# A fused attention and two-layer MLP kernel: the first block's work in another written order

## The chip, the core and the metric

The kernel runs on one core of one Trainium2 chip. The metric is the device time of one execution in microseconds (us), a median over runs. The profiles shown here are each of one execution, and times in them count from the start of its span.

## The reference

```python
def _attn_ref(q, k, v, alpha):                 # q, k, v, alpha: [4, 8, 768, 48]
    for t in range(S):
        state = alpha[:, :, t, :, None] * state + np.einsum('bhd,bhe->bhde', k[:, :, t], v[:, :, t])
        y[:, :, t] = np.einsum('bhd,bhde->bhe', q[:, :, t], state)

def reference(**kwargs):
    x = attention output as [3072 tokens, 384]
    h = x @ w_in                               # [384, 2048]
    x = (h * sigmoid(1.702 * h)) @ w_out       # layer 1
    h = x @ w_in2
    return (h - np.tanh(h)) @ w_out2           # layer 2
```

A linear attention with a decay per channel feeds two MLP layers. The inputs are drawn as float64, and the MLP weights reach the device as 64-bit numbers.

## The kernel before

**Tiles.** Tokens go through each layer in six blocks of 512. The hidden width 2048 is sixteen tiles of 128, numbered m. In one step of a block, `gemm1` (g) makes a hidden tile from the block's tokens, ScalarE applies the gate (`sig_1`, s), and `gemm2` (u) adds the gated tile's share to three accumulating banks of PSUM. Every factor is kept as a high part that TensorE multiplies in one pass and a low remainder, so that each product is three matmuls: a `gemm1` and a `gemm2` are nine matmuls of 128x512 each.

**Gate.** `g_hi` (i) copies the gated tile to its high part on ScalarE, and the low part is the gated tile less the high part: `g_lo` (f) on VectorE. For tiles 6 to 15 of the first block the kernel before uses `g_add` instead: ScalarE writes the negated high part, and an accumulating DMA issued by GpSimd adds the gated tile to it. There are three buffers each for the gated tile, its high and its low part, and two banks of PSUM for `gemm1`.

**Weights.** The weights of hidden tile m (input and output columns together, 768 KB) come by `w_given(m)` (w) on SyncE's DMA queue. They are converted on the device: `w_bits` (b, two VectorE instructions, L172 and L173) and `w_join` (j, L185) build a float32 number, `w_hi` (H, ScalarE, L204) writes the high part and `w_lo` (L, VectorE, L208) the low part. Five buffers (`cf` and two in `xs`) hold the float32 numbers. Layer 1's weights are converted once, all during the first block.

**Attention.** It works in chunks of 128 tokens, 24 in all. Chunks 0 to 3 make the first block's tokens and run ahead of it. Chunks 4 to 7 make the second block's tokens and are worked off between the steps of the first block; for each of them VectorE runs two scans (`a_scan`, p and q), two products (`a_scale`, k) and the state's update (`a_state`, t), TensorE the scores (`s_mm`, S, two halves), the outputs and the state's step (`a_out`, O), ScalarE copies (`s_copy`, `a_guard` d), and GpSimd a masking select for each half of the scores (L310). `a_done` (E) copies the outputs out of PSUM, sends them to memory and reads them back turned (`a_evac`, `a_back`), and then issues the loads of the chunk three further on. `x_hi` and `x_lo` (X, x) split what was read back into the factors of `gemm1`. The later chunks run inside the general loop, whose step s does `gemm1(s)` and `gemm2(s - 3)`.

**Order.** Each engine works off its instructions in the order in which the program is written, up to the last block of layer 1 (`in_order`). A DMA queue's instructions stand in the order of the engine that issues them. In the first block a list of words sets the order: each word is a letter of the table `part` and a number, `g7` being `gemm1` of tile 7. In the list before, the conversion of tile m + 2 or so stands in a row, b, j, H and L one behind the other, next to the step of tile m.

Of the kernel before, what the change touches and what calls it, by code (L numbers as in the profile page):

```python
# [7 lines left out]
F32 = mybir.dt.float32  # L8
# [4 lines left out]
AF = mybir.ActivationFunctionType  # L13
ALU = mybir.AluOpType
# [3 lines left out]
C = 128  # L18
# [50 lines left out]
def linear_attention_mlps(ctx, tc, xq, xv, fa, fv, cst, w1, w2, out):  # L69
    nc = tc.nc  # L70
    V, A, G, P, SP = nc.vector, nc.scalar, nc.gpsimd, nc.tensor, nc.sync
# [22 lines left out]
    glo = [T(f"glo{i}", (128, NB), F32R) for i in range(3)]  # L94
# [28 lines left out]
    for _ in range(2):  # L123
        t = carve(QW)
# [21 lines left out]
    bank = [ps.tile([128, 512], F32, name=f"bank{i}") for i in range(8)]  # L146
# [14 lines left out]
    def w_given(m):  # L161
        SP.dma_start(out=given[m], in_=w1[m].bitcast(I32).rearrange("p (n t) -> p n t", t=2))
# [105 lines left out]
    def a_guard(g):  # L268
        t = (gt if g == 2 else rawf if place_of(g) is spare else arena[:, (QW + VW) * late.index(place_of(g)) :])[:DP, : 2 * AW]
        A.activation(out=t, in_=t, func=AF.Square, accum_out=guard[:, g : g + 1])  # L270
# [157 lines left out]
    def a_back(g):  # L428
        _, xl, o = a_at(g)
        tk = slice(g * C, g * C + C)  # L430
        SP.dma_start(out=xl[:, :, o].bitcast(F32), in_=xt.rearrange("h d t -> (h d) t")[:, tk].rearrange("(k p) t -> p k t", p=128))
# [4 lines left out]
    def x_hi(g, t=None):  # L436
        xh, xl, o = a_at(g)
        A.copy(xh[:, :, o], xl[:, :, o].bitcast(F32) if t is None else x_of(g, t))  # L438

    def x_lo(g, t=None):  # L440
        xh, xl, o = a_at(g)
        V.tensor_tensor(out=xl[:, :, o], in0=xl[:, :, o].bitcast(F32) if t is None else x_of(g, t), in1=xh[:, :, o].bitcast(F32), op=ALU.subtract)  # L442
# [21 lines left out]
    HB = [bank[3], bank[4]]  # L464
# [3 lines left out]
    def gb(s):  # L468
        return gf[s % turn[0]]

    def sig_1(s, h, n):
        A.activation(out=gb(s)[:, :n], in_=h, func=AF.Silu, scale=1.702)  # L472

    def g_hi(s, n):
        A.copy(ghi[s % 3][:, :n], gb(s)[:, :n])  # L475

    def g_lo(s, n):
        V.tensor_tensor(out=glo[s % 3][:, :n], in0=gb(s)[:, :n], in1=ghi[s % 3][:, :n].bitcast(F32), op=ALU.subtract)  # L478

    def g_add(s, n):  # L480
        A.activation(out=glo[s % 3][:, :n], in_=gb(s)[:, :n], func=AF.Copy, scale=-1.0)  # L481
        G.dma_start(out=glo[s % 3][:, :n].bitcast(F32), in_=gb(s)[:, :n], accum_op=ALU.add)

    def g_split(s, n):
        g_hi(s, n)
        g_lo(s, n)
# [49 lines left out]
    LAG = 3  # L536
# [115 lines left out]
    for g in range(3):  # L652
        for r in range(3):
            prep(g + 1, r)
        if g < 2:
            for r in range(2):
                s_mm(g + 1, r, (5, 3)[r])
        if g:
            a_state(g - 1)
        if g < 2:  # L660
            a_out(g, 0)
            idle((4, 3)[g])
        else:
            a_out(2, 0, part=0)
            for r in range(2):
                s_mm(3, r, (5, 3)[r])
            a_out(2, 0, part=1)
        for x in range(2):
            s_copy(g + 1, x, (5, 3)[x], False)
        if g == 2:  # L670
            a_take(2, 0)
        for x in range(2):
            s_copy(g + 1, x, (5, 3)[x], True)
        if g < 2:
            a_evac(g, 0)
            a_guard(g)
            w_given(g + 1)
            a_back(g)
    w_given(3)
    w_given(4)  # L680
    a_load(4)
# [19 lines left out]
    x_hi(2, bank[2])  # L701
    x_lo(2, bank[2])
    w_hi(1, 1)
    x_hi(1)
    x_lo(1)
    w_lo(1, 1)
    x_hi(3, bank[5])
    x_lo(3, bank[5])
    a_guard(3)
    a_load(6)  # L710
    for m in (8, 9, 10):
        w_given(m)
    cv[:] = MT, MT, MT

    steps = [(1, j, m) for j in range(len(L1)) for m in range(MT)] + [(2, j, m) for j in range(len(L2)) for m in range(MT)]
    NS, NS1 = len(steps), len(L1) * MT
# [5 lines left out]
        alt = i >= len(L1) - 1 and (i - len(L1)) % 2  # L722
        return l, j, m, i, t0, n, [bank[b] for b in ((5, 6, 7) if alt else (0, 1, 2))]

    def gate(s):
        sig_1(s, HB[s % 2], NB)
        g_hi(s, NB)
        if s >= 6:
            g_add(s, NB)

    def pads():
        for t in (*late, spare):
            SP.dma_start(out=t[3][DP:], in_=xq[0, : 128 - DP, : NP * C])
# [1 line left out]
    part = {  # L735
        "g": lambda m: gemm1(0, m, HB[m % 2], NB),
        "u": lambda m: gemm2(m, m, bank[:3], NB),
        "h": gate,
        "l": lambda m: g_lo(m, NB),
        "b": lambda m: w_bits(1, m),  # L740
        "j": lambda m: w_join(1, m),
        "H": lambda m: w_hi(1, m),
# [5 lines left out]
        "t": a_state,  # L748
        "d": a_guard,
        "S": lambda n: s_mm(n // 10, n % 10, 5),  # L750
        "C": lambda n: [s_copy(n // 10, n % 10, 5, t) for t in (False, True)],
        "O": lambda g: a_out(g, 5),
        "E": a_done,
        "X": x_hi,
        "x": x_lo,
        "z": lambda _: pads(),
    }
    for word in """
        g0 b2 j2 h0 l0 H2 L2
        g1 u0 b3 h1 l1 j3 H3 L3  # L760
        g2 u1 b4 h2 l2 j4 H4 L4
        g3 u2 b5 h3 l3 j5 H5 L5
        g4 u3 p4 h4 l4 q4 k4 t3
        g5 u4 S40 b6 h5 C40 d4 l5 j6 H6 L6
        u5 S41 C41 g6 b7 j7 h6 H7 L7
        O4 E4 w11 w12 g7 h7 p5 q5 k5 S50 t4 C50
        u6 S51 b8 j8 H8 L8 C51 g8 h8
        u7 X4 d5 b9 j9 H9 L9 x4 g9 h9 O5 E5 z0 w13 w14
        p6 q6 k6 S60 t5 C60 u8 b10 j10 H10 L10 g10 h10
        S61 C61 u9 d6 b11 j11 H11 L11 g11 h11 X5 x5 O6 E6 w15  # L770
        p7 q7 k7 S70 t6 C70 u10 b12 j12 H12 L12 g12 h12
        S71 C71 b13 j13 H13 L13 g13 h13 d7 O7 E7 u11 X6 x6
        b14 j14 H14 L14 g14 h14 p8 q8 u12
        b15 j15 H15 L15 k8 g15 h15 t7 u13 X7 x7
    """.split():
        part[word[0]](int(word[1:]))

    for s in range(MT, NS + LAG):
        if s > MT:
            if s <= NS:  # L780
                l, j, m, i, t0, n, acc = place(s - 1)
                prev = s - 1, n
        if s < NS:
            l, j, m, i, t0, n, acc = place(s)
            h = HB[s % 2][:, :n]
            gemm1(i, m, h, n)
            if l == 2:
                tanh_near(s, h)
        if MT < s <= NS:
            g_split(*prev)  # L790
        if s < NS and l == 1:
            sig_1(s, h, n)
        if s == NS:
            u_flag()
        if s < NS:
            if l == 1 and j + 1 < len(L1):
                t1, n1 = L1[j + 1]
                for c in range(4):
                    steady(t1 // C + c, m - STARTS[c])
            if l == 1 and 0 < j < len(L1) - 1 and m - 2 in STARTS:  # L800
                w_check(1, 4 * (j - 1) + STARTS.index(m - 2))
            if l == 1 and 0 < j < len(L1) - 1 and m in STARTS:
                w_load(1, 4 * (j - 1) + STARTS.index(m), 2)
            if l == 2 and 2 <= j < 4:
                if m % 2:
                    w_check(l, 8 * (j - 2) + m // 2)
                else:
                    tc.keep_in_program_order(w_load(l, 8 * (j - 2) + m // 2))
            if l == 1 and j == len(L1) - 1:
                if m == 0:  # L810
                    for q in range(3):
                        w_load(2, q)
                if m == 1:
                    a_flag()
                if m == 4:
                    x1_load(0)
                if m in (6, 7, 8):
                    x1_split(0, m - 6)
                if m > 0:
                    conv(2, m >= 4)  # L820
            if l == 2:
                if cv[2] < 2 * MT:
                    conv(2)
                if j == 4 and m == 3:
                    w_flag()
                if j + 1 < len(L2):
                    if m == 3:
                        x1_load(j + 1)
                    if m in (6, 7, 8):
                        x1_split(j + 1, m - 6)  # L830
        if s >= LAG:
            l, j, m, i, t0, n, acc = place(s - LAG)
            if s >= NS or s - LAG < 14:
                continue
            gemm2(m, s - LAG, acc, n)
            if m == MT - 1:
                evac(l, t0, n, acc)
        if s == (len(L1) - 1) * MT - 1:
            in_order(begin)


    l, j, m, i, t0, n, acc = place(NS - 1)
# [16 lines left out]
    with tc.If(bad != 0):  # L859
# [20 lines left out]
        for l in (1, 2):  # L880
# [3 lines left out]
            with tc.For_i(0, NTOK, NB) as t0:  # L884
# [7 lines left out]
                for m in range(MT):  # L892
                    h = HB[m % 2]
# [67 lines left out]
```

## Time and profile before

| what | value |
|---|---|
| median of 3 runs | 955.67 us (954.9 to 957.99) |
| the profiled execution | 955.74 us, its span 953.9 us |
| TensorE busy in the span | 916.0 us (96%) |
| VectorE | 664.9 us (70%) |
| ScalarE | 453.7 us (48%) |
| GpSimd | 103.0 us (11%) |

The span is the stretch from the first to the last recorded instruction. A matmul's busy time overlaps that of the next, so a sum over matmuls is longer than the stretch they take: their pace is read from start to start. The first block lies between 33.6 and about 158 us.

### The profile page before, as it was taken

To read this page: it belongs to the slowest core of one execution; us is meant where nothing else is said; L and a number is where in the kernel's file an instruction comes from. 1 tells how busy PE (TensorE), PEld (TensorE's weight loads), DVE (VectorE), ACT (ScalarE), POOL (GpSimd) and SP (SyncE) were. 2 spreads that over 40 slices of the span, in tenths; PEclk is the share of its full clock that TensorE was granted. 3 is DMA by queue.
4 is the path that set the end of the run, shared out by engine and by line. 5 is a ranking of instruction groups with operands and counts; after the bars stand their busy time and mean duration, and the time that the engine had idled before them with its cause. 6 is when DMAs were issued, how large, how long until landed. Compare 5 with 4: busy or idle time off the path is not lost.

```text
span 953.9 us, 13395 instructions
## 1 busy us (share of the span) xinstructions
PE 916.0 (96%) x4941; PEld 721.3 (76%) x4941; DVE 664.9 (70%) x1119; ACT 453.7 (48%) x917; POOL 103.0 (11%) x92
## 2 busy tenths in 40 slices
PE   8987769999999999999999999999999999999996
PEld 5765547877778778777788888888888888888885
DVE  8887547674765767668569976766777777766663
ACT  5545343343434344343444554544656656544542
POOL 5112121110111111110100200100101001000000
PEclk9999889999999999999999999999999999999999
DMA  8955741632444334162625400200432420000001
GB/s 227 292 157 162 220 124 22 198 89 87 129 123 130 84 125 125 58 229 84 215 100 181 151 34 1 100 0 1 133 98 68 165 100 1 34 1 0 34 1 37
DMA packets 57755, 98.23 MB, mean 103 GB/s; under 512 B 5024, under 2 KB 35872, under 8 KB 57680
## 3 DMA queue, kind: packets, MB, share of 16 engines
q1 hardware_dynamic: 55952, 94.27, 31.4%
q0 software_dynamic: 1440, 2.62, 1.6%
q8 instruction: 40, 0.66, 0.3%
q10 hardware_dynamic: 288, 0.40, 0.1%
q14 instruction: 35, 0.29, 0.1%
HBM read 80.88 MB, written 13.76 MB: 99 GB/s over the span
## 4 chain that ended last, share of the span: by engine, by line
PE 88%; DVE 5%; ACT 3%; issue 2%; DMA 1%; SPq 0%; ACTq 0%
PE bank L455 41%; PE bank L461 41%; PE bank L358 2%; PE bank L325 2%; DVE w L208 1%; ACT w L204 1%; PE bank L351 1%; PE bank L296 1%; PE bank L372 1%; DMA xlo<-xt 1%; ACT glo L481 1%; ACT gt L472 1%; DVE xs L185 0%; DMA cs<-cst 0%; DMA xt<-wtb 0%
## 5 line engine op out<-in xcount | busy, mean ns | idle before, releaser
L455 PE MATMUL bank<-xhi,w 128*128 128x512 f32 x1152 | 397.9, 400 | 17.0 <-ACT w L204 11.1
L461 PE MATMUL bank<-ghi,w 128*128 128x512 f32 x1152 | 368.0, 399 | 0.0
L455 PEld LDWEIGHTS bank<-xhi,w 128*128 128x128 f32 x1152 | 217.9, 190 | 75.1 <-ACT w L204 13.8
L461 PEld LDWEIGHTS bank<-ghi,w 128*128 128x128 f32 x1152 | 214.6, 189 | 53.2 <-issue 1.7
L478 DVE TENSOR_TENSOR glo<-gt,ghi 128x512 fp32r<-128x512 f32 x182 | 130.9, 719 | 147.9 <-ACT ghi L475 145.1
L461 PE MATMUL bank<-glo,w 128*128 128x512 f32 x576 | 228.8, 397 | 1.6 <-DVE glo L478 1.6
L455 PE MATMUL bank<-xlo,w 128*128 128x512 f32 x576 | 229.6, 399 | 0.1
L475 ACT CAST ghi<-gt 128x512 fp32r<-128x512 f32 x192 | 118.9, 619 | 205.8 <-DVE gt L496 129.7
L461 PEld LDWEIGHTS bank<-glo,w 128*128 128x128 f32 x576 | 108.6, 189 | 28.8 <-DVE glo L478 2.2
L455 PEld LDWEIGHTS bank<-xlo,w 128*128 128x128 f32 x576 | 109.5, 190 | 26.9 <-DVE xlo L442 0.7
L472 ACT ACTIVATE gt<-bank 128x512 f32<-128x512 f32 x96 | 57.3, 597 | 142.0 <-PE bank L455 141.9
L494 DVE SCALAR_TENSOR_TENSOR arena<-arena,bank 128x512 f32<-128x512 f32 x96 | 65.7, 685 | 31.8 <-ACT arena L492 30.9
L492 ACT ACTIVATE arena<-bank 128x512 f32<-128x512 f32 x96 | 57.2, 596 | 39.1 <-PE bank L455 38.7
L496 DVE SCALAR_TENSOR_TENSOR gt<-arena 128x512 f32<-128x512 f32 x96 | 68.3, 711 | 9.8
L493 ACT ACTIVATE arena<-arena,cs 128x512 f32<-128x512 f32 x96 | 69.6, 725 | 2.9
L495 DVE SCALAR_TENSOR_TENSOR arena<-arena 128x512 f32<-128x512 f32 x96 | 67.9, 707 | 3.1
L533 POOL TENSOR_TENSOR xlo<-arena,xhi 128x512 fp32r<-128x512 f32 x18 | 28.4, 1605 | 339.2 <-ACT xhi L532 339.2
L335 DVE STREAM_TRANSPOSE cf<-arena 32x128 f32<-32x128 f32 x176 | 53.2, 302 | 2.5
L181 ACT ACTIVATE wtb<-wtb 128x768 bf16<-128x768 int16 x32 | 26.8, 837 | 44.3 <-DVE wtb L179 44.3
L442 DVE TENSOR_TENSOR xlo<-xlo,xhi 128x384 fp32r<-128x384 f32 x22 | 13.4, 608 | 44.4 <-ACT xhi L438 44.4
L208 DVE TENSOR_TENSOR w<-cf,w 128x768 fp32r<-128x768 f32 x22 | 23.1, 1048 | 11.2 <-ACT w L204 11.0
L335 DVE STREAM_TRANSPOSE cf<-raw 32x128 f32<-32x128 f32 x80 | 24.2, 302 | 1.1
(139 smaller groups left out, 644.3 us busy)
## 6 DMA issues: line engine op xcount, KB each, us to landing
raw<-w SPq DMA_DIRECT2D x48, 768.0 KB, 4.7
given<-w SPq DMA_DIRECT2D x16, 768.0 KB, 7.9
arena<-xq SPq DMA_DIRECT2D x32, 224.0 KB, 4.9
x1t<-xs SPq DMA_DIRECT2D x6, 768.0 KB, 5.8
arena<-x1t SPq DMA_DIRECT2D x6, 768.0 KB, 4.8
out<-xs SPq DMA_DIRECT2D x17, 256.0 KB, 2.3
xlo<-xt SPq DMA_DIRECT2D x22, 192.0 KB, 2.6
xt<-arena SPq DMA_DIRECT2D x76, 48.0 KB, 1.7
```

The source lines that it names most:

```text
L208: V.tensor_tensor(out=wlo[m], in0=f, in1=whi[m].bitcast(F32), op=ALU.subtract)
L335: V.transpose(out=d[32 * y : 32 * y + 32], in_=k[32 * x : 32 * x + 32, :, 32 * y : 32 * y + 32])
L455: P.matmul(out=h, lhsT=w[m][:, ws], rhs=x[:, k, :n], start=c == 0, stop=c == 3 * KT - 1)
L461: P.matmul(out=acc[k][:, :n], lhsT=w[m][:, ws], rhs=x[s % 3][:, :n], start=m == 0 and c == 0, stop=m == MT - 1 and c == 2)
L472: A.activation(out=gb(s)[:, :n], in_=h, func=AF.Silu, scale=1.702)
L475: A.copy(ghi[s % 3][:, :n], gb(s)[:, :n])
L478: V.tensor_tensor(out=glo[s % 3][:, :n], in0=gb(s)[:, :n], in1=ghi[s % 3][:, :n].bitcast(F32), op=ALU.subtract)
L492: A.activation(out=u, in_=h, func=AF.Square, accum_out=usum[:, s - NS1 :][:, :1])
L493: A.activation(out=w, in_=u, func=AF.Square, bias=pbias)
L494: V.scalar_tensor_tensor(out=p, in0=u, scalar=P3, in1=h, op0=ALU.mult, op1=ALU.mult)
L495: V.scalar_tensor_tensor(out=p, in0=u, scalar=-PR, in1=p, op0=ALU.add, op1=ALU.mult)
L496: V.scalar_tensor_tensor(out=gb(s), in0=w, scalar=PD, in1=p, op0=ALU.add, op1=ALU.mult)
```

## The change

The list of words for the first block is replaced by another one. In it the four parts of a conversion no longer stand in a row; the gate's three parts have words of their own (s, i, f), as have the two kinds of copies of the scores (c, y) and a chunk's load (a). The last preparations ahead of the block (X1, x1, X3, x3, d3, L1, the load of chunk 6, weights 8 to 10) move into the list. `g_add` is dropped: all low parts of the gate are made by VectorE. The first block's `gemm2` of tile 14 moves into the list, and the low part of tile 15 into the loop. Ahead of the block, the load of weights 2 is issued after chunk 1's read-back, no longer before it.

```diff
-    def g_add(s, n):
-        A.activation(out=glo[s % 3][:, :n], in_=gb(s)[:, :n], func=AF.Copy, scale=-1.0)
-        G.dma_start(out=glo[s % 3][:, :n].bitcast(F32), in_=gb(s)[:, :n], accum_op=ALU.add)
...
             a_evac(g, 0)
             a_guard(g)
-            w_given(g + 1)
+            if not g:
+                w_given(1)
             a_back(g)
+    w_given(2)
     w_given(3)
...
     w_hi(1, 1)
-    x_hi(1)
-    x_lo(1)
-    w_lo(1, 1)
-    x_hi(3, bank[5])
-    x_lo(3, bank[5])
-    a_guard(3)
-    a_load(6)
-    for m in (8, 9, 10):
-        w_given(m)
...
-    def gate(s):
-        sig_1(s, HB[s % 2], NB)
-        g_hi(s, NB)
-        if s >= 6:
-            g_add(s, NB)
...
-        g5 u4 S40 b6 h5 C40 d4 l5 j6 H6 L6
-        u5 S41 C41 g6 b7 j7 h6 H7 L7
...
+        H6 g5 p4 s4 i4 t3 u3 s5 q4 i5 L6 g6 f4 f5 b7 u4
+        s6 i6 k4 u5 d4 b8 j8 S40 f6 H8 u6 b9 c40 y40 j7 S41
+        L8 H7 c41 L7 g7 y41 p5 q5 O4 s7 i7 k5 E4 w11 w12 g8
...
     for s in range(MT, NS + LAG):
-        if s > MT:
+        if s:
...
-            if s >= NS or s - LAG < 14:
+            if s >= NS or s - LAG < 15:
```

**VectorE, tiles 2 to 4.** First what stood on VectorE at the head of the block; `given_66` and `given_67` are the weights of tiles 3 and 4, `glo` the gate's low parts, `w_486` the converted tile 2 and `w_513` tile 3.

```order
L185 SCALAR_TENSOR_TENSOR cf_84<-given_65,cf_84 128x768
L478 TENSOR_TENSOR glo_93<-gt,ghi_90 128x512
L208 TENSOR_TENSOR w_486<-cf_84,w_486 128x768
L172 TENSOR_SCALAR xs<-given_66 128x768
L173 SCALAR_TENSOR_TENSOR xs<-given_66,xs 128x768
L478 TENSOR_TENSOR glo_94<-gt,ghi_91 128x512
L185 SCALAR_TENSOR_TENSOR xs<-given_66,xs 128x768
L208 TENSOR_TENSOR w_513<-xs,w_513 128x768
```

Now, with tile 2 as `w_483` and tile 3 as `w_511`:

```order
L442 TENSOR_TENSOR xlo_87<-bank_110,xhi_85 128x3x128
L172 TENSOR_SCALAR xs<-given_66 128x768
L173 SCALAR_TENSOR_TENSOR xs<-given_66,xs 128x768
L208 TENSOR_TENSOR w_483<-cf_84,w_483 128x768
L185 SCALAR_TENSOR_TENSOR xs<-given_66,xs 128x768
L478 TENSOR_TENSOR glo_93<-gt,ghi_90 128x512
L172 TENSOR_SCALAR xs<-given_67 128x768
L173 SCALAR_TENSOR_TENSOR xs<-given_67,xs 128x768
L478 TENSOR_TENSOR glo_94<-gt,ghi_91 128x512
L208 TENSOR_TENSOR w_511<-xs,w_511 128x768
```

Tile 3's L208 stood directly behind its own L185; now a low part and the next tile's first two instructions stand between, and tile 2's L208 has moved behind the start of tile 3.

**VectorE, tiles 13 and 14.** `given_76` and `given_77` are the weights of tiles 13 and 14. Before:

```order
L172 TENSOR_SCALAR xs<-given_76 128x768
L173 SCALAR_TENSOR_TENSOR xs<-given_76,xs 128x768
L185 SCALAR_TENSOR_TENSOR xs<-given_76,xs 128x768
L208 TENSOR_TENSOR w_1007<-xs,w_1007 128x768
L442 TENSOR_TENSOR xlo_88<-xlo_88,xhi_86 128x3x128
L172 TENSOR_SCALAR xs<-given_77 128x768
```

Now:

```order
L172 TENSOR_SCALAR xs<-given_77 128x768
L173 SCALAR_TENSOR_TENSOR xs<-given_77,xs 128x768
L478 TENSOR_TENSOR glo_95<-gt,ghi_92 128x512
L172 TENSOR_SCALAR xs<-given_76 128x768
L173 SCALAR_TENSOR_TENSOR xs<-given_76,xs 128x768
L185 SCALAR_TENSOR_TENSOR xs<-given_76,xs 128x768
```

Tile 14's first instructions now stand ahead of tile 13's, and ahead of the gate's low part of tile 11.

**SyncE's queue ahead of the block.** `xt` is the memory through which a chunk's outputs go, `xlo` what is read back, `given_65` the weights of tile 2. The piece of the difference:

```order
 L431 DMA xlo_87<-xt 128x3x128
 L421 DMA xt<-wtb 48x2x128 x4
+L431 DMA xlo_87<-xt 128x3x128
 L162 DMA given_65<-w 128x1536
-L431 DMA xlo_87<-xt 128x3x128
 L162 DMA given_66<-w 128x1536
```

Chunk 1's read-back and the load of weights 2 have changed places; the order of all further loads and trips on this queue is the same in both kernels.

## Rows read from the trace of the kernel before

**Rows 1.** Stretches: length, busy PE, PEld, DVE, ACT, POOL; clock, DMA share, GB/s.

```profile
35.95:57.50 21.55, 21.29 (x91) 16.38 (x89) 18.37 (x25) 10.25 (x16) 0.00 (x0) 1.00 1.06 302
116.70:158.31 41.61, 31.85 (x163) 22.83 (x162) 22.73 (x39) 15.45 (x30) 7.68 (x8) 0.87 0.38 99
160.00:940.00 780.00, 780.00 (x4054) 624.30 (x4053) 547.58 (x940) 376.64 (x737) 67.70 (x47) 1.00 0.27 88
```

**Rows 2.** TensorE's groups by line, 35.95 to 158.31 us: count, busy, idle before.

```profile
L455 PE MATMUL bank<-xhi,w 128*128 128x512 f32 x102 | 41.0, 459 | 15.2 <-ACT w L204 11.1 <-DVE w L208 3.4 <-DVE seg L257 0.5
...
L455 PE MATMUL bank<-xlo,w 128*128 128x512 f32 x52 | 22.6, 435 | 0.1
L461 PE MATMUL bank<-glo,w 128*128 128x512 f32 x45 | 18.6, 413 | 1.6 <-DVE glo L478 1.6
L296 PE MATMUL bank<-arena 48*128 48x176 f32 x48 | 5.9, 367 | 8.1 <-issue 5.5 <-ACT glo L481 2.1 <-DVE arena L266 0.5
```

**Rows 3.** VectorE's waits, 35.95 to 158.31 us: total, times, longest.

```profile
DVE w L208 <- ACT w L204: 22.2, 14, 4.5
```

**Rows 4.** Chain that ended last: start us, us, what (pieces, in time).

```profile
63.32 0.80 PE bank L296 x8
...
112.75 4.14 PE bank L461 x9
...
231.40 1.09 PE bank L325 x16
...
236.87 2.09 PE bank L461 x9
```

**Rows 5.** Timeline of TensorE, outputs of chunk 4: start us, us, instruction.

```profile
66.34 0.66 PE L351 MATMUL bank<-arena,state 48*48 48x128 f32 x16
...
67.83 0.53 PE L372 MATMUL bank<-arena 128*48 128x48 f32 x16
```

**Rows 6.** Timeline of VectorE: start us, us, instruction [idle before].

```profile
33.20 0.56 DVE L442 TENSOR_TENSOR xlo<-xlo,xhi 128x384 fp32r<-128x384 f32 x1 [1.97 <-ACT xhi L438]
...
55.21 0.68 DVE L478 TENSOR_TENSOR glo<-gt,ghi 128x512 fp32r<-128x512 f32 x1
55.80 1.23 DVE L261 TENSOR_TENSOR_SCAN arena<-arena,seg 112x516 f32<-112x516 f32 x1
...
60.26 1.12 DVE L478 TENSOR_TENSOR glo<-gt,ghi 128x512 fp32r<-128x512 f32 x1
...
69.89 0.06 DVE L257 MEMSET seg<- 112x4 f32 x1
...
74.48 0.56 DVE L172 TENSOR_SCALAR xs<-given 128x768 int32<-128x768 int32 x1
...
111.28 0.55 DVE L172 TENSOR_SCALAR cf<-given 128x768 int32<-128x768 int32 x1
...
114.72 0.96 DVE L208 TENSOR_TENSOR w<-cf,w 128x768 fp32r<-128x768 f32 x1 [0.90 <-ACT w L204]
115.60 0.55 DVE L172 TENSOR_SCALAR xs<-given 128x768 int32<-128x768 int32 x1
...
141.63 2.98 DVE L208 TENSOR_TENSOR w<-cf,w 128x768 fp32r<-128x768 f32 x1 [0.90 <-ACT w L204]
```

**Rows 7.** Timeline of GpSimd, near two of the instructions of rows 6.

```profile
60.00 0.83 POOL L310 TENSOR_SCALAR_AFFINE_SELECT arena<-arena 128x512 f32<-128x512 f32 x1 [32.73 <-ACT arena L308]
...
142.30 1.49 POOL L266 TENSOR_TENSOR arena<-arena 112x512 f32<-112x512 f32 x1
```

**Rows 8.** SyncE's queue, the trip of chunk 5 and weights 13 and 14.

```profile
91.43 2.90 SPq L421 DMA_DIRECT2D xt<-wtb  x4
...
100.28 1.55 SPq L162 DMA_DIRECT2D given<-w  x2
```

**Rows 9.** Time to landing of weights 13 and 14 (issues 100 to 103 us).

```profile
DMA to landing us min/median/max: 7.0/7.3/7.6
```

**Rows 10.** Time to landing of weights 5 and 6 (issues 32 to 35 us).

```profile
DMA to landing us min/median/max: 11.9/12.9/13.9
```

More of the change, by code (lines that the diff above doesn't have):

```diff
@@ L737, in linear_attention_mlps @@
         "u": lambda m: gemm2(m, m, bank[:3], NB),
-        "h": gate,
-        "l": lambda m: g_lo(m, NB),
+        "s": lambda m: sig_1(m, HB[m % 2], NB),
+        "i": lambda m: g_hi(m, NB),
+        "f": lambda m: g_lo(m, NB),
         "b": lambda m: w_bits(1, m),
@@ L750, in linear_attention_mlps @@
         "S": lambda n: s_mm(n // 10, n % 10, 5),
-        "C": lambda n: [s_copy(n // 10, n % 10, 5, t) for t in (False, True)],
+        "c": lambda n: s_copy(n // 10, n % 10, 5, False),
+        "y": lambda n: s_copy(n // 10, n % 10, 5, True),
         "O": lambda g: a_out(g, 5),
         "E": a_done,
-        "X": x_hi,
-        "x": x_lo,
+        "a": a_load,
+        "X": lambda g: x_hi(g, bank[5] if g == 3 else None),
+        "x": lambda g: x_lo(g, bank[5] if g == 3 else None),
         "z": lambda _: pads(),
@@ L758, in linear_attention_mlps @@
     for word in """
[L759 to L763, printed above, removed]
-        g5 u4 S40 b6 h5 C40 d4 l5 j6 H6 L6
-        u5 S41 C41 g6 b7 j7 h6 H7 L7
[L766 to L774, printed above, removed]
+        X1 L1 X3 d3 a6 w8 w9 w10 x1 b2 j2 x3 g0 H2 b3 g1
+        s0 i0 L2 j3 g2 s1 f0 H3 b4 i1 u0 s2 f1 i2 L3 j4
+        g3 f2 H4 b5 u1 s3 i3 L4 j5 u2 b6 H5 L5 g4 j6 f3
+        H6 g5 p4 s4 i4 t3 u3 s5 q4 i5 L6 g6 f4 f5 b7 u4
+        s6 i6 k4 u5 d4 b8 j8 S40 f6 H8 u6 b9 c40 y40 j7 S41
+        L8 H7 c41 L7 g7 y41 p5 q5 O4 s7 i7 k5 E4 w11 w12 g8
+        t4 d5 f7 j9 S50 s8 p6 H9 u7 c50 L9 y50 i8 q6 S51 g9
+        c51 k6 y51 f8 O5 s9 b10 X4 i9 j10 E5 z0 w13 w14 u8 t5
+        H10 f9 d6 p7 S60 u9 c60 L10 y60 q7 S61 b11 g10 c61 y61 j11
+        b12 H11 O6 s10 i10 L11 X5 j12 g11 E6 w15 f10 H12 k7 u10 s11
+        i11 t6 d7 x4 L12 S70 g12 b14 c70 y70 f11 S71 b13 s12 i12 u11
+        c71 j13 y71 X6 f12 H13 O7 x6 L13 x5 E7 j14 g13 b15 H14 u12
+        s13 L14 i13 j15 f13 H15 g14 p8 L15 u13 s14 i14 q8 X7 f14 k8
+        g15 x7 t7 u14 s15
     """.split():
@@ L788, in linear_attention_mlps @@
                 tanh_near(s, h)
-        if MT < s <= NS:
+        if s <= NS:
             g_split(*prev)
```

## The prediction

> **What bounds the kernel now.** I read the stretches first, then TensorE's groups by line inside the first block, then the waits of the engines it waits for, last the timelines. From 160 to 940 us TensorE has no free moment: 780.00 of 780 us busy at full clock [rows 1]. So whatever the first block takes longer or shorter shifts the end by as much. At the block's head it is nearly as dense, 21.29 of 21.55 us. Between 57.5 and 158 us it is not: in the last stretch of the block it is busy 31.85 of 41.61 us at a mean clock of 0.87 [rows 1].
>
> How much is lost? I take the stretch from 35.95 us, where `gemm1` of tile 1 starts, to 158.31 us, where the loop's `gemm1` of tile 2 of the second block starts: 122.4 us. In it lie `gemm1` of steps 1 to 17 and `gemm2` of tiles 0 to 14, 32 times nine matmuls; the counts 102, 52 and 45 of the groups agree [rows 2]. Nine matmuls at full pace are 2.09 us [rows 4], so 66.9 us. The attention between them: eight halves of scores at 0.80 [rows 4], 6.4; outputs of four chunks, of which chunk 4's takes 66.34 to 68.36, 2.0 us [rows 5], two of the others leaving a part out, about 7.0 in all; chunk 8's whole scores 1.09 [rows 4]. Together 81.4 us. The loss is 41.0 us. About 25 of it are idle (15.2, 0.1, 1.6 and 8.1 us ahead of the groups); the rest, some 16, is matmuls at half pace, such as nine in 4.14 us where 2.09 is usual [rows 2, 4]. The clock that the rows grant falls after such idle stretches.
>
> What TensorE waits for is the conversion: of 15.2 us ahead of `gemm1`, 11.1 end with the high part of a weight (L204) and 3.4 with its low part (L208) [rows 2]. VectorE itself waits in the same place: 14 times, 22.2 us, for ScalarE's high part before it can make the low one [rows 3], since the two stand next to each other in the order: join, then 0.90 us idle, then the low part [rows 6]. While it waits, the next chunk's scans and products wait behind it, and TensorE's 5.5 us "issue" ahead of a half of scores is of that kind [rows 2].
>
> **The change, part by part.**
>
> The new order. Between a tile's join and its low part now stands other VectorE work in all 14 cases of tiles 2 to 15 (for tile 7 only one low part, 0.9 us). So the 22.2 us should nearly go. What remains is either TensorE's own 81.4 us or VectorE's work without waits, whichever is longer. VectorE's work up to the low part of tile 14's gate, from rows: a tile's five instructions 115.60 - 111.28 - 0.90 = 3.42 us, 14 tiles, 47.9; a low part of the gate 55.80 - 55.21 = 0.59, 15 of them, 8.9; a chunk's scans, products and state 74.48 - 69.89 = 4.59, four chunks, 18.4; chunk 8's two scans of 1.23 and small parts 2.7; five splits of 0.56, 2.8 [rows 6]. Sum 80.7 us. Where does it start? Before, x1 began at 33.20 after 1.97 us of waiting [rows 6]. The low part of weight 1 now fills 0.96 of that wait, so x1 can begin between 32.2 and 33.2; I take 32.5. VectorE is then through at 113.2. Behind it come `gemm2` of tile 14, `gemm1` of steps 16 and 17 and the whole scores: 3 x 2.09 + 1.09 = 7.4, so step 18 starts at 120.6. TensorE alone would allow 35.95 + 81.4 = 117.4. **VectorE is the bound, by about 3 us**, and what delays it from here counts nearly in full.
>
> All low parts by VectorE. Ten more instructions of 0.59 us, 5.9 us, are in the sum already. What goes: ten copies on ScalarE and ten accumulating transfers. ScalarE is busy 15.45 of 41.61 us in the last stretch [rows 1], so its share is worth nothing by itself. The accumulated part came late, but `gemm2` runs two or three steps behind in either order, so I give this nothing either. If VectorE were the only bound, this edit alone would cost 5.9 us; the removed waits are its cover.
>
> Chunk 1's read-back ahead of weights 2. The read-back should land earlier, and x1 with it. But b2 and j2, 2.5 us, now stand ahead of x3, which the last three matmuls of the first `gemm1` need; so the block's start on TensorE stays where it was, within 0.5 us either way. The gain is the start of VectorE above, no more.
>
> `gemm2` of tile 14 in the list, the last low part in the loop: the same instructions in nearly the same place, nothing; beside them lies TensorE's saturated stretch.
>
> What the new density costs:
> - GpSimd. A low part that met a masking select took 1.12 instead of 0.68 us [rows 6], while the select ran 0.83 us from 60.00 [rows 7]. Eight selects lie in the block; at 0.4 each 3.2 us. Bounds: nothing, if they fall on other moments, and 8 x 0.83 = 6.6.
> - Chunk 8's products on GpSimd. A low part of a weight beside them took 2.98 instead of 0.96 us [rows 6], until the second product was through at 143.8 [rows 7]. Now they meet the last weight or the last low parts of the gate: 2.0 us, between 0 and 3.0 (two products of 1.49).
> - Late weights. Weights 13 and 14 are issued behind chunk 5's trip; from the trip's first write at 91.43 to their landing were about 17.4 us (last issue near 101.4, [rows 8], 7.3 us to land, [rows 9]). In the new order chunk 5's outputs are done after 17 times 2.09, four halves of scores and two outputs, 42 us behind the start, near 79; with small waits the first write is at 80.8, and weight 14 lands at 98.2. VectorE has 64 us of work ahead of it, and with five selects reaches it near 98.7. It is that close, and tile 14 stands ahead of 13 in the new order, in front of a low part that TensorE needs. I take 1.0. Below: 0. Above: the landing of weights 5 and 6, on a loaded queue, was up to 13.9 us [rows 10], 6.3 more.
> - Waits between ScalarE and VectorE that remain: 1.0, bounds 0 and 14 x 0.90 = 12.6.
>
> Sum: 120.6 + 3.2 + 2.0 + 1.0 + 1.0 = 127.8 against 158.3, a gain of 30.5. The profiled execution, 955.74, lies on the median, 955.67. **Forecast 925.2 us.**
>
> **The rivals.**
>
> A, weights become the bound. If the later trips run on a queue as loaded as at the block's head, weight 14 is some 6 us late, weight 15 another 2, and TensorE, idle meanwhile, loses about 2 more at half pace, as the nine matmuls in 4.14 show [rows 4, 10]. 925.2 + 6 + 2 + 2 less the 1.0 already counted: 934. For it: all loads have to come up to 30 us earlier. Against it: the share of transfers in the last stretch was 0.38 [rows 1].
>
> B, GpSimd holds VectorE fully. The 2.98 us row ended only after GpSimd's second product [rows 6, 7]. If each select keeps a VectorE instruction waiting for its whole 0.83 us, the selects cost 6.6 and the products 3.0, which is 4.4 more: 929.6. The Trainium skill, in "SBUF — State Buffer", section "Who interferes with whom", says that a VectorE instruction with two inputs in SBUF and a GpSimd instruction that reads SBUF do not share their port but block one another, whichever comes second waiting to the end. By that rule 6.6 is the ceiling, not the mean, and the 1.12 us row, which lost 0.44 of 0.83, fits an instruction that came half way through.
>
> C, slower than before: the trips run one behind the other. If chunk 5's outputs came to stand behind weight 12, and chunk 6's behind 14, each of the three trips would cost 17.4 us, two conversions 6.8, a `gemm1` and a `gemm2` 4.2 and outputs 1.5, thus 29.9. From a first write near 70, weight 15 lands at 70 + 2 x 29.9 + 17.4 = 147; with its conversion, `gemm1` of tile 15 and the 7.4 us behind, step 18 starts at 160, and with one loaded landing (6.3) at 166.5: 964. It decides if VectorE reaches something of chunk 7 or of weight 11 before what chunk 5's outputs need. In the new order these stand behind, by VectorE's work about 3 us later than the outputs, so little speaks for it.
>
> D, nothing happens: 955.7, if something later than the block had its own fixed pace. The 780.00 of 780 us speaks against it.
>
> **How the numbers follow.** Forecast 0.70, with 917 to 932 as its own range; A 0.13, B 0.09, C 0.04, D 0.04. The low end is TensorE's bound, 955.7 - 41.0 = 915. The high end is 939: rival A with some of the 12.6 us of remaining waits. Under 0.3%, or 2.9 us, a measurement here could hardly tell from no change; faster by more than that 0.92, within it 0.04, slower 0.04.
>
> **What would show it.** In the profile after, step 18 starts near 128 us, TensorE's idle ahead of `gemm1` in the block is below 6 us instead of 15.2, and its clock stays at 1.0 through the block. VectorE is over 90% busy from 33 to 113 us; its wait for L204 falls from 22.2 to below 3. The first wait to look for is that of L172 for weight 14. The prediction is wrong if VectorE has gaps of several us in front of loads (A), if its instructions are longer by more than 5 us in all (B), or if the stretch behind the block is no longer dense.

## The result, and the profile after

The changed kernel takes 923.96 us (median of 6 runs, 922.34 to 925.82) against 956.47 us for the kernel before on the same chips (6 runs, 954.09 to 957.99). The ratio is 0.9665, with a 95% interval of 0.9646 to 0.9684. The forecast was 925.2 us, in a range of 915 to 939.

The stretches of the changed kernel come first (columns as in [rows 1]).

```profile
35.95:57.50 21.55, 21.55 (x94) 17.46 (x94) 21.27 (x31) 10.65 (x17) 0.00 (x0) 1.00 1.05 310
57.50:85.20 27.70, 27.54 (x200) 20.19 (x199) 27.23 (x40) 17.44 (x43) 6.46 (x5) 1.00 0.40 133
85.20:116.70 31.50, 27.76 (x192) 20.50 (x191) 25.08 (x35) 16.47 (x36) 5.54 (x5) 1.00 0.72 207
116.70:130.00 13.30, 13.29 (x106) 10.17 (x104) 12.88 (x29) 5.72 (x11) 2.84 (x3) 1.00 0.08 31
130.00:900.00 770.00, 768.94 (x3972) 615.50 (x3968) 541.14 (x931) 371.57 (x727) 67.29 (x47) 1.00 0.28 89
```

TensorE, first number behind the length, is now dense in the whole first block except for some 4 us between 85 and 117 us, and its clock, the third number from the end, is 1.00 throughout. Behind 130 us it is as saturated as in [rows 1], so the block's gain goes through to the end. Where does the block end? TensorE's timeline has the start of step 17's `gemm1`, and the first wait behind it:

```profile
123.53 0.50 PE L455 MATMUL bank<-xhi,w 128*128 128x512 f32 x1
...
136.69 0.73 PE L461 MATMUL bank<-ghi,w 128*128 128x512 f32 x2 [1.06 <-ACT xs L516]
```

Step 17 starts at 123.53, so step 18 starts nine matmuls (2.2 us) later, at 125.73; before it was 158.31. Of these 32.6 us a new wait for the evacuation L516 gives 1.1 back, and the span falls from 953.9 to 922.5, by 31.4.

TensorE's groups by line in the block, 35.95 to 125.73 us, answer to [rows 2]; the waits of VectorE, 31.65 to 118.5 us, to [rows 3].

```profile
L455 PE MATMUL bank<-xhi,w 128*128 128x512 f32 x102 | 35.7, 407 | 1.8 <-DVE w L208 1.7 <-DVE seg L257 0.2
...
L455 PE MATMUL bank<-xlo,w 128*128 128x512 f32 x54 | 21.1, 396 | 2.1 <-DVE xlo L442 2.1
L461 PE MATMUL bank<-glo,w 128*128 128x512 f32 x45 | 18.0, 400 | 2.1 <-DVE glo L478 2.1
L296 PE MATMUL bank<-arena 48*128 48x176 f32 x48 | 5.2, 335 | 0.0
```

```profile
DVE xs L172 <- DMA given<-w: 3.7, 1, 3.7
DVE cf L172 <- DMA given<-w: 2.9, 2, 2.4
```

The same 102 matmuls of the first line were busy 41.0 us before and waited 15.2; now 35.7 and 1.8. The wait for ScalarE's high part L204, 22.2 us on VectorE and 11.1 on TensorE, is gone altogether. What VectorE waits for now is weights: 14, 15 and, at the head, 2. Its timeline shows where:

```profile
98.78 0.56 DVE L172 TENSOR_SCALAR xs<-given 128x768 int32<-128x768 int32 x1 [3.72 <-DMA given<-w]
...
109.48 0.56 DVE L172 TENSOR_SCALAR cf<-given 128x768 int32<-128x768 int32 x1 [2.38 <-DMA given<-w]
```

TensorE's two waits inside the block stand right behind these: 2.06 us at 101.43 for the low part behind weight 14, and 1.68 us at 111.96 for L208.

### The profile page after: what moved, and what is told of

It is laid out like the page before. It is cut to its first block, busy times and chain, and to the rows that moved or that the text cites. A ratio compares the mean times of both kernels' runs of the same rounds, so it can differ in the third digit from the quotient of the medians.

```text
span 922.5 us, 13368 instructions
## 1 busy us (share of the span) xinstructions
PE 905.8 (98%) x4941; PEld 716.2 (78%) x4941; DVE 668.6 (72%) x1129; ACT 449.5 (49%) x907; POOL 98.5 (11%) x82
## 4 chain that ended last, share of the span: by engine, by line
PE 86%; DVE 8%; DMA 3%; issue 1%; ACT 1%; SPq 0%; DVEq 0%; ACTq 0%
PE bank L461 41%; PE bank L455 39%; DMA given<-w 2%; PE bank L358 2%; PE bank L325 2%; PE bank L619 1%; DVE glo L478 1%; PE bank L351 1%; DVE cf L173 1%; DVE cf L335 1%; DVE w L208 1%; DVE arena L261 1%; PE bank L372 1%; DVE arena L258 1%; DVE cf L185 1%
## 5 line engine op out<-in xcount | busy, mean ns | idle before, releaser
L455 PE MATMUL bank<-xhi,w 128*128 128x512 f32 x1152 | 392.3, 395 | 2.4 <-DVE w L208 1.7
L478 DVE TENSOR_TENSOR glo<-gt,ghi 128x512 fp32r<-128x512 f32 x192 | 136.3, 710 | 148.0 <-ACT ghi L475 145.9
L475 ACT CAST ghi<-gt 128x512 fp32r<-128x512 f32 x192 | 118.9, 619 | 204.0 <-DVE gt L492 130.2
L472 ACT ACTIVATE gt<-bank 128x512 f32<-128x512 f32 x96 | 57.3, 597 | 116.2 <-PE bank L455 112.2
L442 DVE TENSOR_TENSOR xlo<-xlo,xhi 128x384 fp32r<-128x384 f32 x22 | 14.5, 660 | 26.0 <-ACT xhi L438 26.0
L265 POOL TENSOR_TENSOR arena<-arena 112x512 f32<-112x512 f32 x11 | 14.0, 1272 | 118.0 <-DVE seg L259 86.9
L310 POOL TENSOR_SCALAR_AFFINE_SELECT arena<-arena 128x512 f32<-128x512 f32 x16 | 18.4, 1161 | 70.7 <-ACT arena L308 62.8
```

Of the source, the lines that this page charges most:

```text
L455: P.matmul(out=h, lhsT=w[m][:, ws], rhs=x[:, k, :n], start=c == 0, stop=c == 3 * KT - 1)
```

## The experiments

Twelve kernels ran. Medians are of the kernel's runs, ratios against the kernel before on the same chip, brackets 95% intervals.

**The order without VectorE's low parts.** `order_dma_low` keeps the new list and gives the low parts of tiles 6 to 14 back to ScalarE and the accumulating DMA.

```diff
-        "i": lambda m: g_hi(m, NB),
-        "f": lambda m: g_lo(m, NB),
+        "i": lambda m: [g_hi(m, NB)] + [g_add(m, NB) for _ in range(m >= 6)],
+        "f": lambda m: g_lo(m, NB) if m < 6 else None,
```

> The new order, with the low parts of tiles 6 to 14 made again by ScalarE and an accumulating transfer of GpSimd, right behind the high part. Theory (the order is the gain, the removed transfers are worth little by themselves): VectorE does 5.3 us less, but a low part lands some 5.4 us behind its high part (0.62 + 0.86 + 3.9), which in five of the nine tiles is later than gemm2 comes (4.2, 4.3, 3.7, 3.0 and 3.3 us behind the high part), together some 8 us of waiting; net 926 to 931. Rival (the removed transfers are the main source): 940 or more.

Measured: 938.46 us, ratio 0.9826 [0.9803, 0.9849]. This lies between the two, nearer to the rival. TensorE's waits from 60 to 160 us, in the profiled execution (943.46 us, the longest of the five), have one large row:

```profile
PE bank L461 <- DMA glo<-gt: 12.8, 5, 4.3
```

The matmuls with the low part wait five times for the transfer, up to 4.3 us each, and the granted clock of 85 to 117 us is 0.78. So in the new order dropping these nine transfers is worth some 14.5 us against the changed kernel's 923.96.

**VectorE's low parts without the order.** `old_order_ve_low` is the kernel before with one line changed in `gate`.

```diff
         if s >= 6:
-            g_add(s, NB)
+            g_lo(s, NB)
```

> The kernel before with its own order, all low parts of the first block by VectorE, in the gate's place. Theory (the order is the gain): the conversions' waits stay, VectorE has 5.9 us more and now also waits for the high part of the gate behind TensorE, but gemm2 no longer waits for the transfers; 948 to 960. Rival (the removed transfers are the main source): 940 or less.

Measured: 974.79 us, ratio 1.0205 [1.0181, 1.0229]: slower, which neither theory said. VectorE's waits from 36 to 165 us, and its timeline at one of them:

```profile
DVE glo L478 <- ACT ghi L475: 36.7, 10, 5.7
```

```profile
80.06 0.96 DVE L208 TENSOR_TENSOR w<-xs,w 128x768 fp32r<-128x768 f32 x1 [0.90 <-ACT w L204]
86.68 0.69 DVE L478 TENSOR_TENSOR glo<-gt,ghi 128x512 fp32r<-128x512 f32 x1 [5.66 <-ACT ghi L475]
87.29 0.55 DVE L172 TENSOR_SCALAR xs<-given 128x768 int32<-128x768 int32 x1
```

The low part itself takes 0.69 us. But it stands on VectorE right behind the gate, ahead of the next tile's conversion (L172), and waits there 5.66 us for ScalarE, which waits for TensorE (here 3.13 us for a half of scores, then 1.30 us for `gemm1`); and TensorE's next `gemm1` waits 3.29 us for that conversion. It is a ring of three engines with one step in it at a time. My theory formed after this run: what costs time is not which engine makes the low part, but what it stands in front of.

**Only the place of the low parts.** `old_order_late_low` tests this. The order and all else are those of before, and the low parts of tiles 6 to 15, by VectorE, stand directly ahead of the `gemm2` that needs them.

```diff
-        u6 S51 b8 j8 H8 L8 C51 g8 h8
+        l6 u6 S51 b8 j8 H8 L8 C51 g8 h8
...
-        b15 j15 H15 L15 k8 g15 h15 t7 u13 X7 x7
+        b15 j15 H15 L15 k8 g15 h15 t7 l13 u13 l14 X7 x7 l15
```

> The kernel before's order, the gate's low parts of tiles 6 to 15 of the first block by VectorE as in old_order_ve_low, but each placed directly ahead of the gemm2 that needs it instead of directly behind ScalarE's high part. Theory (old_order_ve_low was slow because its low parts stood on VectorE ahead of the next conversion and waited 3 to 6 us for ScalarE's high part of the gate): the waits of L478 for L475, 41.5 us there, nearly vanish, and the time is 945 to 958 us instead of 974.8. Rival (the ten more instructions on VectorE cost the time, wherever they stand): 968 us or more.

Measured: 951.94 us, ratio 0.9965 [0.995, 0.998], as the theory said; from 36 to 165 us the wait of L478 for L475 falls from 36.7 us in ten pieces to 1.3 in one. The same instructions on the same engine, two or three steps later: 22.8 us.

**Only the place of the conversions.** `old_order_spread` is the kernel before with the next tile's first two conversion instructions between a high part and its low part.

```diff
-        g1 u0 b3 h1 l1 j3 H3 L3
+        g1 u0 h1 l1 j3 H3 b4 L3
...
-        u6 S51 b8 j8 H8 L8 C51 g8 h8
+        u6 S51 j8 H8 b9 L8 C51 g8 h8
```

> The kernel before, with one thing moved: in tiles 2 to 14 the first two conversion instructions of the next tile (b) stand between ScalarE's high part (H) and the low part (L), so that VectorE has 1.1 us of work while ScalarE writes the high part. The gate's low parts stay with ScalarE and the accumulating DMA. Theory (the wait of a low part for its high part is part of the loss, but the smaller one; the rest comes from where the conversion stands against the steps): the 0.90 us waits of L208 for L204 go, 12 to 14 times 0.9, and the time falls to 942 to 950 us, not to the 938 of the new order with DMA low parts. Rival (ScalarE's high part is late because TensorE, and not VectorE, is late): the waits move to another instruction and the time stays at 953 to 957.

Measured: 947.83 us, ratio 0.9928 [0.9904, 0.9953], in the theory's range. The kernel before had fourteen waits for L204, eight of them of 0.90 us. Those go, but 16.6 us stay in eight pieces, five of them of 1.8 to 4.1 us. A gap of 0.90 us, about ScalarE's own time for the high part, can be filled on VectorE; in a longer one ScalarE itself comes late.

**Both.** `old_order_spread_late` makes the two edits at once.

> Both edits at once in the kernel before's order: the next tile's first two conversion instructions between high and low part of a weight, and the gate's low parts by VectorE directly ahead of their gemm2. Theory (the new order gains by these two things together, and the rest of its 32 us by running tiles further ahead): 930 to 942 us, below each of the two alone. Rival (the two gains are the same gain, or one undoes the other): not below the better of the two alone.

Measured: 942.62 us, ratio 0.9879 [0.9847, 0.991]. It lies 0.6 us above the forecast's range. The two gains, 7.5 and 3.3 us, add up within the noise: 12.7 us of the changed kernel's 32.

**The splits later.** `old_order_turn_late` moves X and x of chunks 4 to 6 as well.

```diff
-        l7 u7 X4 d5 j9 H9 b10 L9 x4 g9 h9 O5 E5 z0 w13 w14
+        l7 u7 d5 j9 H9 b10 L9 g9 h9 O5 E5 z0 w13 w14
...
-        S61 C61 l9 u9 d6 j11 H11 b12 L11 g11 h11 X5 x5 O6 E6 w15
+        X4 x4 S61 C61 l9 u9 d6 j11 H11 b12 L11 g11 h11 O6 E6 w15
```

> old_order_spread_late (942.62 us) with the splits of chunks 4 to 6 (X and x: what was read back from memory, split into factors) one to two steps later in the order. In its trace VectorE still stood 11.6 us in three waits of L442 for ScalarE's L438, which itself waited for the trip through memory, and the next chunk's scans and scores (5.0 us of TensorE waiting) stood behind one of them. Theory (an in-order VectorE waits for the trip, and that is a third part of the loss besides the weight's and the gate's low parts): the 11.6 us nearly go and the time is 930 to 937 us. Rival (the trips are off the path, what ends last is the conversion directly ahead of its own step): 940 to 944 us.

Measured: 938.99 us, ratio 0.9847 [0.9819, 0.9875], between the two (the intervals don't separate it from 942.62), and my reason was wrong. VectorE still waits 10.2 us for splits. Its timeline, and ScalarE's at the same place:

```profile
109.62 0.56 DVE L442 TENSOR_TENSOR xlo<-xlo,xhi 128x384 fp32r<-128x384 f32 x1 [3.67 <-ACT xhi L438]
...
120.86 0.96 DVE L208 TENSOR_TENSOR w<-xs,w 128x768 fp32r<-128x768 f32 x1 [4.11 <-ACT w L204]
```

```profile
107.93 0.60 ACT L472 ACTIVATE gt<-bank 128x512 f32<-128x512 f32 x1 [3.67 <-PE bank L455]
108.56 0.62 ACT L475 CAST ghi<-gt 128x512 fp32r<-128x512 f32 x1
109.08 0.51 ACT L438 CAST xhi<-xlo 128x384 fp32r<-128x384 f32 x1
...
117.26 0.60 ACT L472 ACTIVATE gt<-bank 128x512 f32<-128x512 f32 x1 [5.35 <-PE bank L455]
```

ScalarE's L438 waits for no transfer. It stands behind the gate L472, which waited 3.67 us for TensorE's `gemm1`, and VectorE's split then waits the same 3.67. The high part L204, at 119.99, stands behind the next gate in the same way. The other two waits of splits, behind gates that waited 3.42 and 4.02 us, are alike. The trip through memory was not the cause; it is the ring again, by way of ScalarE's order.

**Conversions a whole step earlier.** `old_order_ahead` also converts tile m + 1 ahead of `gemm1` of tile m.

```diff
-        l6 u6 S51 j8 H8 b9 L8 C51 g8 h8
+        l6 u6 S51 j9 H9 b10 L9 C51 g8 h8
...
-        j15 H15 L15 k8 X6 x6 g15 h15 t7 l13 u13 l14 X7 x7 l15
+        k8 X6 x6 g15 h15 t7 l13 u13 l14 X7 x7 l15
```

> old_order_turn_late with the conversions of tiles 6 to 15 one step earlier, so that tile m + 1 is converted ahead of gemm1 of tile m instead of tile m directly ahead of its own gemm1. Theory (what is left of the loss is TensorE waiting for L204 of the very tile that it is about to multiply): TensorE's waits for L204 and L208 go below 2 us and the time is 922 to 930 us, the changed kernel's 924 within a per cent, reached in the kernel before's order by four named moves. Rival (one step further ahead on five buffers only makes VectorE wait for weights or buffers): no less than old_order_turn_late.

Measured: 940.62 us, ratio 0.9865 [0.9848, 0.9881]: the rival's time. Its reason holds in part, since VectorE waits 3.8 us for weights here. TensorE's waits from 31 to 160 us:

```profile
PE bank L296 <- issue: 9.1, 3, 3.6
PE bank L461 <- DVE glo L478: 5.1, 3, 2.5
PE bank L296 <- DVE arena L266: 2.7, 1, 2.7
```

The waits for weights are gone from TensorE, as the theory asked, and the scores (L296) and low parts have taken their place, by my reading because VectorE now comes too late for them (of the 9.1 us "issue" the profile names no releaser). One step of lead for one kind of work is paid by another kind.

**Chunk 1's trip.** `trip_back` undoes this part of the change alone.

```diff
-            if not g:
-                w_given(1)
+            w_given(g + 1)
             a_back(g)
-    w_given(2)
```

> The changed kernel with the load of weights 2 again ahead of chunk 1's read-back. Theory: x1 starts up to 1.5 us later, and VectorE is behind by about 1 us up to tile 14, where it waits 3.72 us for weights anyway, so that the delay vanishes there: 924, within 0.7 us. Rival (the start counts in full): 925 to 926.

Measured: 924.41 us, ratio 0.9696 [0.9674, 0.9718], no difference. SyncE's queue in the changed kernel, then in `trip_back`:

```profile
27.68 0.40 SPq L431 DMA_DIRECT2D xlo<-xt  x1
28.12 1.44 SPq L162 DMA_DIRECT2D given<-w  x3
```

```profile
23.51 0.43 SPq L162 DMA_DIRECT2D given<-w  x1
28.99 0.40 SPq L431 DMA_DIRECT2D xlo<-xt  x1
29.44 0.96 SPq L162 DMA_DIRECT2D given<-w  x2
```

In the kernel before the read-back was issued at 27.60. It leaves only when the write of the same trip has landed (SyncE waits 3.0 us for that in the kernel before, 3.8 in the changed one, 4.9 in `trip_back`), so moving the weights behind it does not bring its issue forward; it only sends weight 2 off at 28.12 instead of 23.51, in time that the queue would have waited anyway. Its landing is another matter. ScalarE's split of it, in the kernel before and in the changed one:

```profile
32.66 0.51 ACT L438 CAST xhi<-xlo 128x384 fp32r<-128x384 f32 x1 [1.84 <-DMA xlo<-xt]
```

```profile
30.37 0.53 ACT L438 CAST xhi<-xlo 128x384 fp32r<-128x384 f32 x1
```

From issue to landing the read-back took 5.0 us in the first and 2.4 in the second. Ten of the fourteen profiled kernels, the kernel before among them, have weight 2 ahead of it: in seven it took 2.5 to 3.0 us, in three (the kernel before, `old_order_late_low`, `early_x3_trip`) 5.0 to 5.3, and x1 then waited 1.7 to 2.4 us. In the four with weight 2 behind it, it took 2.4 to 2.6. Four are too few to show that the move prevents the late landing.

**Weights earlier.** `weights_early` issues the loads of weights 11 to 15 right behind weight 10.

```diff
-        X1 L1 X3 d3 a6 w8 w9 w10 x1 b2 j2 x3 g0 H2 b3 g1
+        X1 L1 X3 d3 a6 w8 w9 w10 w11 w12 w13 w14 w15 x1 b2 j2 x3 g0 H2 b3 g1
```

> The changed kernel with the loads of weights 11 to 15 issued right behind that of weights 10, instead of behind the trips of chunks 4 to 6. Theory (VectorE's waits of 3.72 and 2.38 us for weights 14 and 15 are what TensorE's waits of 2.06 and 1.68 us come from): both waits go, 919.5 to 921.5. Rival (the loads then fill the queue up to the first trip and delay chunk 7's load and the read-backs): 923 to 927.

Measured: 919.57 us, ratio 0.9629 [0.961, 0.9649], as the theory said. All of VectorE's waits for weights but the first are gone; VectorE's and TensorE's gaps of 85 to 117 us go with them:

```profile
85.20:116.70 31.50, 31.50 (x212) 24.39 (x211) 30.98 (x41) 18.52 (x42) 8.16 (x6) 1.00 0.54 146
```

**The head of the block.** Three kernels on top of `weights_early`: `early_x3_first` writes x3 ahead of b2 and j2, `early_trip_back` also undoes chunk 1's trip, and `early_x3_trip` does both.

```diff
-        X1 L1 X3 d3 a6 w8 w9 w10 w11 w12 w13 w14 w15 x1 b2 j2 x3 g0 H2 b3 g1
+        X1 L1 X3 d3 a6 w8 w9 w10 w11 w12 w13 w14 w15 x1 x3 b2 j2 g0 H2 b3 g1
```

> The changed kernel with the loads of weights 11 to 15 issued behind weight 10 (weights_early, 919.57 us) and x3 ahead of b2 and j2 at the block's head. Theory (VectorE's x3 behind b2 and j2 is what the first gemm1's last three matmuls wait for, 2.1 to 2.6 us): that wait goes, gemm1 of tile 1 starts up to 2 us earlier, and, as VectorE's own work is only exchanged in order, between nothing and 2 us of it reach the end: 917.5 to 919.5. Rival (VectorE's sum alone sets the end of the block): 919.0 to 920.5, no difference to weights_early.

```diff
-            if not g:
-                w_given(1)
+            w_given(g + 1)
             a_back(g)
-    w_given(2)
```

> weights_early (919.57 us) with the load of weights 2 ahead of chunk 1's read-back again, as in the kernel before. In trip_back the same edit to the changed kernel moved nothing measurable. Theory (there the delay of x1 was hidden by the 3.5 us that VectorE waited for weight 14 later; without that wait nothing hides it): about 1 us more, 920 to 921.5. Rival (the read-back isn't late on the queue either way, or another wait at the block's head hides it): 919.0 to 920.0.

> weights_early (919.57 us) with both later edits: x3 ahead of b2 and j2, and the load of weights 2 ahead of chunk 1's read-back. Each alone brought 918.5 and 918.3. Theory (both save the same thing, VectorE's wait of 0.5 to 1.0 us for weights 2, and VectorE's sum sets the end of the block, so that TensorE's earlier start is worth nothing): 917.9 to 918.9. Rival (the two save different things, VectorE's wait and TensorE's 1.5 us for x3): 916.5 to 917.5.

Measured: 918.54 us, ratio 0.962 [0.9606, 0.9633]; 918.3, 0.9618 [0.9604, 0.9631]; 918.08, 0.9628 [0.9614, 0.9641]. The first lies where its theory put it, though not for the reason given there, and the second fits neither forecast: undoing the trip costs nothing even without cover, and if anything gains. The third fits, the two do not add; its profile is of the longest execution, 919.97 us, and has the late landing of the read-back. VectorE's first conversion in `weights_early`, then in `early_trip_back`:

```profile
33.27 0.56 DVE L172 TENSOR_SCALAR cf<-given 128x768 int32<-128x768 int32 x1 [0.99 <-DMA given<-w]
```

```profile
32.26 0.57 DVE L172 TENSOR_SCALAR cf<-given 128x768 int32<-128x768 int32 x1
```

It starts 1.0 us earlier because weight 2 is there, and the time is 1.3 us lower, which the intervals alone don't separate (the profile of `weights_early` is of its longest execution, 920.52 us). `early_x3_first` covers the same wait with x3: its L172 starts at 32.75. There TensorE's second `gemm1` begins at 34.41 and step 18 at 120.92, in `early_trip_back` at 36.14 and 120.57. TensorE's earlier start is worth nothing: 1.1 us of it go into waits for VectorE and ScalarE (0.2 in `early_trip_back`), and VectorE's first low part of the gate starts at the same time in both, 38.4. What both save is, by these rows, VectorE's wait for weight 2.

## Why the prediction was right, and where it was not

**What bounds.** The saturation behind the block held, 768.94 of 770 us, and carried 31.4 of the block's 32.6 us. TensorE's own work was mis-sized: `early_trip_back` has in the block one wait of 0.2 us on TensorE and takes from 36.14 to 120.57 us, 84.4 us, where I had counted 81.4. The attention in it takes 14.4 us, as counted (14.5). It is the matmuls beside it that take longer: nine between two halves of scores 2.30 us from start to start in the changed kernel, not the 2.09 of [rows 4].

```profile
62.57 0.73 PE L461 MATMUL bank<-ghi,w 128*128 128x512 f32 x2
...
64.87 0.87 PE L296 MATMUL bank<-arena 48*128 48x176 f32 x8
```

The loss was 38 us, not 41 (some 13 instead of 16 at half pace), and the floor some 918 instead of 915. The last three experiments stand on it.

"VectorE is the bound, by about 3 us" did not hold. In `early_trip_back`, where weights come in time, VectorE's low part ahead of `gemm2` of tile 14 ends at 112.18:

```profile
111.52 0.66 DVE L478 TENSOR_TENSOR glo<-gt,ghi 128x512 fp32r<-128x512 f32 x1
```

With 7.3 us behind it, VectorE would allow step 18 at 119.5, and TensorE starts it at 120.57: the two engines are within about 1 us of each other. In the changed kernel VectorE was the later one because it waited for weights, and of its delay not nearly all counted: 6.1 us of waits for weights 14 and 15 became 3.7 us of waits on TensorE.

**The new order.** That the 22.2 us of waits would go was right. The reason given was too small: I saw only that join, high part and low part stand next to each other. `old_order_spread` removes exactly that in tiles 2 to 14 and gains 7.5 us. The larger part of the waits, which the prediction did not name, is the ring: whatever on VectorE needs a ScalarE instruction that stands behind the newest gate waits for TensorE. In four of the kernel before's five longer waits L204 stands behind a gate that itself waited 1.3 to 4.6 us for `gemm1`. VectorE's splits waited so too, as a row of VectorE's waits in the kernel before (36 to 160 us) has it, a wait that my sum removed unnamed by counting work alone:

```profile
DVE xlo L442 <- ACT xhi L438: 16.1, 3, 7.0
```

In the changed kernel this wait is 0.5 us. Three edits of the kernel before's order reach 939 us, the fourth gained nothing, and which of the remaining moves of the list bring the other 15 us was not taken apart; that the ring is what these undo is my reading, not shown.

**VectorE's sum.** Predicted: start 32.5, work 80.7, then 7.4 on TensorE. Measured: x1 starts at 31.65, the last low part ahead of `gemm2` of tile 14 starts at 117.80 and ends at 118.46, and step 18 starts 7.3 us later. Of the 86.8 us between, 6.6 are the waits of the rows above and some 3.4 what GpSimd costs, so the work itself is 76.8, 3.9 less than predicted. 2.3 of it are in the conversions (last section) and 0.7 in a chunk's state that now comes behind; 0.9 I could not place.

**Late weights, 1.0 us: mis-sized.** They cost 3.7 and 2.4 us of VectorE's time and some 4 of the kernel's, by `weights_early` (4.4 by the medians, 3.4 by the ratios). The place was as forecast, and so was the trip: its first write came at 80.73 (forecast 80.8) and weight 14 was there at 98.8 (98.2). It is VectorE that arrived at 95.1 instead of 98.7, mostly since its work was shorter. So the two errors are one, and cancel: a shorter sum met a fixed date. That the forecast came within 1.2 us is in part luck: the waits for weights were 5.6 us longer than the 1.0 in the sum, and the start (0.9), the work (3.9), GpSimd (1.8) and the remaining waits (1.0) came out 7.6 us lower, so that step 18 came at 125.73 instead of 127.8. Rival A was this mechanism at twice the price.

**GpSimd.** Selects: predicted 3.2 us; six of the eight hit, for 0.31 to 0.44 us each, 2.4 in all. Chunk 8's products: predicted 2.0, measured 1.0 for L261, ahead of the last low part, and 1.0 for L442 behind it. Rival B fell on the selects, which hit but overlap in part only. (The row of 1.12 us that I took for half way began 0.26 us into a select of 0.83.)

**All low parts by VectorE.** The 5.9 us in the sum are right, but "I give this nothing either", for the ten transfers, failed most: in the new order nine of them would cost some 14.5 us, by `order_dma_low`. A transfer that is covered at the old pace, where `gemm2` came three slow steps later, is not at the new one; it also landed later there, a median of 5.6 us after its issue instead of 3.9. And at its old place VectorE's low part would have cost 19.5 us. Neither half of the change alone gives what both give: 17 gained, 19.5 lost, and 32 gained together.

**Chunk 1's trip.** Against the profile of the kernel before, the read-back did land earlier, as forecast, at 30.1 us instead of 32.6, and x1 started at 31.65 instead of 33.20. But the move did not make its issue earlier, and it is not shown to be the cause: the 1.97 us of waiting, from which I took VectorE's start, was a late landing, which seven of ten profiles with the old order of these loads don't have. In `early_trip_back`, one of the seven, x1 starts at 31.79.

**The signs named** were seen: step 18 at 125.73 (near 128), 3.9 us of idle ahead of `gemm1` (below 6), clock 1.00, VectorE busy 79.1 of 86.8 us (91%), no wait for L204, and, after a short wait for weight 2, that of L172 for weight 14. Rivals C and D found nothing: chunk 5's outputs came first, and nothing later had a pace of its own.

## What to carry to other kernels

Look at what stands behind a waiting instruction on its own engine, not at the wait's length: moving low parts by two or three steps on the same engine was worth 22.8 us, filling the gaps of 0.90 us between high and low parts 7.5. Where in-order engines hand one tile around, a lead for one kind of work can pass the wait on to the next, as in `old_order_ahead`; the new list moves all kinds together. And ask of each transfer with a fixed date whether its user now comes before it: here five loads issued earlier gave another 4 us or so, and with the head of the block put right 918 us is the best version measured.

## What the runs showed of the hardware

**A conversion is shorter when another tile's instruction stands behind it.** VectorE's timeline of the changed kernel, twice L173 and what follows it:

```profile
33.31 0.96 DVE L173 SCALAR_TENSOR_TENSOR cf<-given,cf 128x768 int32<-128x768 int32 x1
34.30 0.96 DVE L185 SCALAR_TENSOR_TENSOR cf<-given,cf 128x768 int32<-128x768 int32 x1
...
36.23 0.96 DVE L173 SCALAR_TENSOR_TENSOR xs<-given,xs 128x768 int32<-128x768 int32 x1
37.10 0.95 DVE L208 TENSOR_TENSOR w<-cf,w 128x768 fp32r<-128x768 f32 x1
```

Followed by its own join, which reads its result, L173 takes 0.99 us from start to start; followed by another tile's work 0.87. L185 likewise takes 0.87 when the next instruction needs nothing of it, and its full 0.95 where VectorE then waited. The new order has 9 of 14 pairs apart, so about 14 x 0.09 + 9 x 0.12 = 2.3 us come from this.

**VectorE beside GpSimd.** The timelines of VectorE and of GpSimd at chunk 8's products:

```profile
115.65 2.23 DVE L261 TENSOR_TENSOR_SCAN arena<-arena,seg 112x516 f32<-112x516 f32 x1
...
118.38 1.54 DVE L442 TENSOR_TENSOR xlo<-xlo,xhi 128x384 fp32r<-128x384 f32 x1
```

```profile
114.75 2.03 POOL L265 TENSOR_TENSOR arena<-arena 112x512 f32<-112x512 f32 x1 [13.93 <-DMA arena<-xq]
117.95 1.55 POOL L266 TENSOR_TENSOR arena<-arena 112x512 f32<-112x512 f32 x1 [1.17 <-DVE arena L261]
```

L261, 1.23 us elsewhere, began while GpSimd's product ran and ended 1.10 us after the product's end at 116.78; L442, 0.56 elsewhere, ended 0.42 after the second product's end at 119.50. Both look as if they ran only once GpSimd was through. The Trainium skill, "SBUF — State Buffer", section "Who interferes with whom", says that a VectorE instruction with two inputs in SBUF and a GpSimd instruction that reads SBUF contend for an exclusive lock, and the one that comes second waits to the end of the first; these rows agree within 0.15 us.
